# Moving three gradient half-pieces into the last spectral pair and two norm quarters, with x1's gradient in a tile of its own

## The chip, the cores and the metric

The kernel runs on one core of one Trainium2 chip. The metric is the device time of the whole program in microseconds (us), the median over several runs. Engines: TensorE (PE) multiplies matrices, VectorE (DVE) and ScalarE (ACT) work elementwise, GpSimd (POOL) and SyncE (SP) issue the DMAs here.

## The reference, cut to what matters

The program computes one transformer-like block and its full gradient: the output, and the gradients of x, two spectral filters, W1, b1, W2, b2, the conditioning vector c and the modulation matrix.

```python
mod = (_silu(c) @ w_mod).reshape(c.shape[0], 6, 1, -1)
sa, ca, ga, sb, cb, gb = ...
h = _layernorm(x, axis=-1) * (1 + ca) + sa
x = x + ga * _A_ref(h, A_w_r, A_w_i)          # rfft2, times a complex filter, irfft2
h = _layernorm(x, axis=-1) * (1 + cb) + sb
x = x + gb * _B_ref(h, B_w1, B_b1, B_w2, B_b2) # layernorm, W1, gelu, W2
...
_out, _vjp = jax.vjp(_f, A_x, A_w_r, A_w_i, B_w1, B_b1, B_w2, B_b2, c, w_mod)
_grads = _vjp(grad_out)
```

S = 2048 tokens, D = 1024 channels, F = 3584 hidden channels; everything that is stored is bf16.

## The kernel before

The kernel keeps 128 tokens or channels on the partitions. Both Fourier transforms are matrix products with cosine and sine tables. Symmetry splits each into four classes (CE, SE, CO, SO: even and odd cosines and sines), and the token axis is worked in four quarters of 512 tokens that are folded onto one another.

The forward part and the MLP's backward part come first; the change lies in the last 270 us. There `spectral_core(False, ...)` runs the spectral block backward:

- `s_fwd` makes four tables U with the token-axis products.
- Eight pairs follow (`pair(n, ...)`). Each multiplies its frequencies with the filters on VectorE and writes two rows groups of R. After pair n the callback `beside_bwd(n)` runs. Pair 7 completes R.
- `s_inv` makes the inverse token-axis products (L565, named `pv`): CE and SE after pair 5, CO and SO after pair 7. They read the tables smA2 and smB2 (tags `sma`, `smb`) and R.
- Four quarters i follow. The `po` products (L630) of a quarter are 32 small matmuls, evicted by L635 and L637 into `o4`, a slice of the tile `ct`. Then `consume_bwd(i, ...)` unfolds `o4` (L173), loads x's rows into `n1` (a tile `xt`, two of them in turn, tags `sma` and `px0`), normalises them on ScalarE (`norm_act`, L461), takes the layer norm backward row group by row group (L1185 and `ln_bwd`, L1032 to L1037), loads the gradient that comes from x1 into `n1` again (L1188), adds it (L1189) and stores the result (`store_tok`: one DMA on SP and two indirect ones on POOL).

Independent work for TensorE is laid between these steps by hand. `pieces()` is a generator: each `next` writes down one piece, and `fill(n)` draws n of them. A piece is 16 matmuls of 128x512: half of a 128-row block of W2's gradient (L1071, named `gw2acc`), or a 128x512 block of W1's gradient (L1252, named `gw1acc`). Numbered from 0 in the order of drawing, pieces 0 to 47 are W2 halves, pieces 48 to 51 are the last four W2 halves, cut by token quarter so that each frees one of the tiles gB, and pieces 52 to 107 are W1 blocks. Some pieces also write down loads: those of W2 load the hidden activations two blocks ahead (`hh_load`, L1214, a transposing DMA), and piece 52 loads the normalised tokens (`n3n`, L1237, into the tags t0 to t3 that the pairs' temporaries held) and calls `gw1_load` twice (L1203). Each `gw1_load` is two transposing DMAs of 1 MB into two of the four tiles `gzh`, which take the places of the four gB tiles. Every eighth W1 piece calls it again for the group after the next.

Drawn before the change: 12 pieces ahead of the pairs, 32 beside them (`fill(1)` four times per pair), 8, 8, 10 and 10 in the quarters (`fill((6, 6, 8, 8)[i])`, the column sums `halves_sum` on TensorE (L196), `fill(2)`), 8 with each of three modulation-gradient rows (`gmod_row`), and 4 at the end.

The tile framework's scheduler does not keep the written order strictly. Among instructions of one engine that it holds to be ready it takes the one written first; a tile that shares a tag waits until the last reader of the tile before it is done. `tc.issue_after(ins)` puts instructions behind `ins` on its engine. SP and POOL run their queues in order: an instruction that waits holds up all behind it.

Of the kernel before, what the change touches and what calls it, by code (L numbers as in the profile page):

```python
# [11 lines left out]
BF16 = mybir.dt.bfloat16  # L12
I32 = mybir.dt.int32
ACT = mybir.ActivationFunctionType
ALU = mybir.AluOpType
AX = mybir.AxisListType

P = 128
S = 2048
D = 1024  # L20
# [15 lines left out]
def kernel(  # L36
# [24 lines left out]
    nc = tc.nc  # L61
# [4 lines left out]
    reg = ctx.enter_context(tc.tile_pool(name="reg", bufs=1))  # L66
# [6 lines left out]
    def ps_s(name):  # L73
        return psum.tile([P, 512], FP32, tag="s", name=name)
# [31 lines left out]
    d_gx1 = dram.tile([S, D], BF16, name="d_gx1")  # L106
# [13 lines left out]
    def chunk_rows(dt, i):  # L120
        return dt[4 * i * P:4 * (i + 1) * P, :].rearrange("(q p) d -> p q d", p=P)

    def tok_flat(ap):
        return ap[0] if len(ap.shape) == 3 else ap

    def load_tok(t4, src, i, eng=None):
        s3 = tok_flat(src)
        ins = (eng or nc.sync).dma_start(out=t4[:, 0:4:3, :],
                          in_=bass.AP(tensor=s3.tensor, offset=s3.offset + 128 * i * D, ap=[[D, P], [1024 * D, 2], [1, D]]))
        for q in range(2):  # L130
            nc.gpsimd.indirect_dma_start(out=t4[:, 1 + q, :], out_offset=None, in_=s3,
                                         in_offset=bass.IndirectOffsetOnAxis(ap=xidx[:, 2 * i + q:2 * i + q + 1], axis=0))
        return ins
# [11 lines left out]
    def store_tok(dst, t4, i):  # L145
        s3 = tok_flat(dst)
        nc.sync.dma_start(out=bass.AP(tensor=s3.tensor, offset=s3.offset + 128 * i * D, ap=[[D, P], [1024 * D, 2], [1, D]]),
                          in_=t4[:, 0:4:3, :])
        for q in range(2):
            nc.gpsimd.indirect_dma_start(out=s3, out_offset=bass.IndirectOffsetOnAxis(ap=xidx[:, 2 * i + q:2 * i + q + 1], axis=0),  # L150
                                         in_=t4[:, 1 + q, :], in_offset=None)
# [20 lines left out]
    def tt(out, a, b, op):  # L172
        return nc.vector.tensor_tensor(out=out, in0=a, in1=b, op=op)  # L173
# [24 lines left out]
    def halves_sum(acc, src4, first, last):  # L198
        for i in range(4):
            for h in range(2):  # L200
                strip_sum(acc, h + 2 * (i % 2), src4[:, i, h * KH:(h + 1) * KH], first and i < 2, last and i >= 2)
# [7 lines left out]
    def store_halves(acc, row, spent4, r):  # L209
        odd = spent4[0:64, 0, :].bitcast(FP32)  # L210
        nc.scalar.copy(out=odd, in_=acc[64:128, :])
        tt(row, acc[0:64, :], odd, ALU.add)
        store_strips(row, 0, r)
# [63 lines left out]
    def unfold_d(o4, tmp):  # L277
        n = o4.shape[1]
        ov = o4.rearrange("p c (a b w) -> p c a b w", b=2, w=256)
        tv = tmp.rearrange("p c (s b w) -> p c s b w", s=2, w=256)  # L280
        tt(tv[:, :, 0], ov[:, :, :, 0, :], ov[:, :, :, 1, :], ALU.add)
        tt(tv[:, :, 1], ov[:, :, :, 0, :], ov[:, :, :, 1, :], ALU.subtract)
        fwd = o4.rearrange("p c (b w) -> p c b w", w=512)[:, :, :, 0:256]
        rev = bass.AP(tensor=o4.tensor, offset=o4.offset + 1023, ap=[o4.ap[0], [D, n], [-512, 2], [-1, 256]])
        tt(fwd, tv[:, :, :, 0, :], tv[:, :, :, 1, :], ALU.add)
        tt(rev, tv[:, :, :, 0, :], tv[:, :, :, 1, :], ALU.subtract)

    def unfold_tok(o4, tmp):
        tt(tmp[:, 0:4:2, :], o4[:, 0:4:2, :], o4[:, 1:4:2, :], ALU.add)
        tt(tmp[:, 1:4:2, :], o4[:, 0:4:2, :], o4[:, 1:4:2, :], ALU.subtract)  # L290
        tt(o4[:, 0:4:3, :], tmp[:, 0:2, :], tmp[:, 2:4, :], ALU.add)
        tt(o4[:, 1:3, :], tmp[:, 0:2, :], tmp[:, 2:4, :], ALU.subtract)
# [165 lines left out]
    def norm_act(out4, in4, row, i):  # L458
        for q in range(4):
            t = 4 * i + q  # L460
            nc.scalar.activation(out=out4[:, q, :], in_=in4[:, q, :], func=ACT.Identity,  # L461
                                 scale=stats[:, row, 0, t:t + 1], bias=stats[:, row, 1, t:t + 1])
# [567 lines left out]
    def ln_bwd(g_in, gsum, n_ap, rstd, out_ap, tmp):  # L1030
        sc = small.tile([P, 4], FP32, tag="lbsc", bufs=4)
        nc.vector.tensor_tensor_reduce(out=tmp, in0=g_in, in1=n_ap, scale=1.0, scalar=0.0,  # L1032
                                       op0=ALU.mult, op1=ALU.add, accum_out=sc[:, 1:2])
        nc.vector.tensor_scalar(out=sc[:, 2:3], in0=gsum, scalar1=rstd, scalar2=-1.0 / D, op0=ALU.mult, op1=ALU.mult)
        nc.vector.tensor_scalar(out=sc[:, 3:4], in0=sc[:, 1:2], scalar1=rstd, scalar2=-1.0 / D, op0=ALU.mult, op1=ALU.mult)
        nc.scalar.activation(out=tmp, in_=n_ap, func=ACT.Identity, scale=sc[:, 3:4], bias=sc[:, 2:3])
        nc.vector.scalar_tensor_tensor(out=out_ap, in0=g_in, scalar=rstd, in1=tmp, op0=ALU.mult, op1=ALU.add)  # L1037
# [127 lines left out]
    hh_o = [None, None] + [4, 5, 6, 7, 4, 5] + [0, 1] + [2, 0, 1] * 6  # L1165
    css2 = reg.tile([P, 2, 2, 2 * PW], BF16, name="cs01b", tag="px0")
    nc.gpsimd.memset(css2[:], 0.0)
    accCA = []

    def consume_bwd(i, o4, tmp, tmp2, n1):  # L1170
        if i == 0:
            accCA.append(ps_s("accCA"))
            nc.vector.tensor_copy(out=sacc, in_=o4[:, 0, :])
        else:
            tt(sacc, sacc, o4[:, 0, :], ALU.add)
        unfold_d(o4, tmp)
        unfold_tok(o4, tmp)
        load_tok(n1, A_x, i)
        with tc.issue_after(last_po[0].ins):
            norm_act(n1, n1, 0, i)  # L1180
        tt(tmp, o4, n1, ALU.mult)
        s1c = small.tile([P, 4], FP32, tag="s1c")
        for q in range(4):
            t = 4 * i + q
            nc.vector.tensor_tensor_reduce(out=o4[:, q, :], in0=o4[:, q, :], in1=opca_row, scale=1.0, scalar=0.0,  # L1185
                                           op0=ALU.mult, op1=ALU.add, accum_out=s1c[:, q:q + 1])
            ln_bwd(o4[:, q, :], s1c[:, q:q + 1], n1[:, q, :], stats[:, 0, 0, t:t + 1], o4[:, q, :], tmp2[:, q, :])
        nc.sync.dma_start(out=n1, in_=chunk_rows(d_gx1, i))  # L1188
        tt(o4, o4, n1, ALU.add)  # L1189
        store_tok(out_1, o4, i)  # L1190
        fill((6, 6, 8, 8)[i])
        halves_sum(accCA[0], tmp, i == 0, i == 3)
        fill(2)
        if i == 3:
            rows = small.tile([P, D], BF16, tag="gmrow", bufs=1)
            store_halves(accCA[0], rows[0:64, 0:KH], tmp, 1)
# [10 lines left out]
    def gmod_row(r, ins):  # L1207
        with tc.issue_after(ins.ins):
            for _ in gmod_steps(r, w1g["wr"], w1g["gw"], w1g["gr"][:, r % 2, :]):
                pass  # L1210
# [52 lines left out]
    def fill(n):  # L1263
        for _ in range(n):
            next(todo)
        done[0] += n
# [21 lines left out]
    def beside_bwd(n):  # L1288
        for k in range(4):
            fill(1)  # L1290
            if 3 - k < (1, 2, 2, 2, 2, 2, 3, 3)[n]:
                with tc.issue_after(hh_in[0].ins):
                    next(rows34)

    spectral_core(False, fbuf2, (smA2, smB2), em2, [css2[:, 0], css2[:, 1]],
                  new_pair_temps(["t0", "t1", "t2", "t3"]), act_copy, s_copy, act_copy, consume_bwd, "fr", pfs, fill, mid_bwd, beside_bwd)


# [7 lines left out]

    for r in (2, 1, 0):
        gmod_row(r, w1g["ins"])
        fill(8)
    fill(NFC * 4 - done[0])  # L1310
    fin2 = reg.tile([P, 2, P], BF16, name="fin2", tag="gm")
    make_identity(nc, fin2[:, 0, :])
# [40 lines left out]
```

## Time and profile before

| | us |
|---|---|
| median of 3 runs | 1466.65 (1458.96, 1466.65, 1467.49) |
| the profiled execution, its own time | 1469.58 |
| its span, first to last instruction | 1467.6 |
| TensorE busy | 1397.0 (95%) |
| VectorE busy | 1073.8 (73%) |
| ScalarE busy | 718.0 (49%) |
| GpSimd busy | 365.7 (25%) |
| mean granted TensorE clock | 0.987 |

The lines of a timeline give the start and length in us, engine, source line, operation, the tile written and the tiles read, a count, and in brackets the engine's idle time before it with what ended that. Lines of windows give for a stretch its length, then the busy time and count of PE, PEld (weight loads), DVE, ACT and POOL, then the granted TensorE clock as a share of full speed, the busy share of the DMA engines and GB/s. A line of waits has the total, the number of waits and the longest.

### The profile page before, as it was taken

How to read it: one execution, taken by the hardware profiler on the slowest of the kernel's cores; microseconds unless marked ns; L12 is line 12 of the kernel's file. 1: busy time of each engine (PE TensorE's matmuls, PEld its weight loads, DVE VectorE, ACT ScalarE, POOL GpSimd, SP SyncE). 2: the span in 40 equal slices, each digit the busy share in tenths (PEclk: the TensorE clock that was granted, in tenths of full speed). 3: DMA queues.
4: the chain of work that ended last, by engine and by line, in shares of the span. 5: the costliest groups of instructions: out<-in, count | busy, mean ns of one | idle time of the engine just before them, and what ended most of it. 6: DMA issues, size and time to landing. Idle time of an engine off the chain costs nothing. (4 is left out here: it accounts for less than half of the span.)

```text
span 1467.6 us, 18265 instructions
## 1 busy us (share of the span) xinstructions
PE 1397.0 (95%) x6703; PEld 652.8 (44%) x6835; DVE 1073.8 (73%) x1581; ACT 718.0 (49%) x953; POOL 365.7 (25%) x441
## 2 busy tenths in 40 slices
PE   5889999999999999999989999999999999899997
PEld 2434545444444434444434444444444445444443
DVE  5883787898799787887520789888467578898542
ACT  4765556757886666665302333342623434444211
POOL 6610541211112122122211011021245431222432
PEclk8999999999999999999999999999999999999999
DMA  9972573899886876696999275396699987766992
GB/s 333 284 229 58 145 243 131 267 240 333 243 252 219 248 247 226 209 293 210 241 306 253 82 261 183 120 267 170 186 223 256 255 212 215 196 180 179 290 249 103
DMA packets 358366, 324.27 MB, mean 221 GB/s; under 512 B 209386, under 2 KB 301056, under 8 KB 358022
## 3 DMA queue, kind: packets, MB, share of 16 engines
q1 hardware_dynamic: 324166, 207.71, 52.1%
q0 software_dynamic: 34112, 115.41, 22.6%
q8 instruction: 53, 0.87, 0.2%
q14 instruction: 35, 0.29, 0.1%
HBM read 162.06 MB, written 111.20 MB: 186 GB/s over the span
## 5 line engine op out<-in xcount | busy, mean ns | idle before, releaser
L684 PE MATMUL pp<-gBoT,wt 128*128 128x512 bf16 x878 | 197.4, 381 | 5.7 <-DMA wt<-in_B_w_dram 2.7
L948 PE MATMUL pg<-w1T,gzr 128*128 128x512 bf16 x876 | 194.6, 379 | 1.6 <-ACT gn3b L956 0.2
L1252 PE MATMUL gw1acc<-gzh,n3n 128*128 128x512 bf16 x876 | 194.0, 379 | 1.2 <-DMA gzh<-d_gz 0.2
L802 PEld LDWEIGHTS <-w 128*128 128x128 bf16 x896 | 87.3, 98 | 111.7 <-issue 7.6
L684 PEld LDWEIGHTS <-wt 128*128 128x128 bf16 x896 | 87.9, 98 | 110.0 <-issue 5.2
L948 PEld LDWEIGHTS <-gzr 128*128 128x128 bf16 x896 | 86.8, 98 | 107.8 <-issue 4.7
L1252 PEld LDWEIGHTS <-n3n 128*128 128x128 bf16 x896 | 87.6, 98 | 105.3 <-issue 1.9
L802 PE MATMUL pz<-n3Ta,w 128*128 128x512 bf16 x437 | 98.8, 381 | 6.0 <-DVE w2sD L873 2.7
L1071 PE MATMUL gw2acc<-gB,hhsA 128*128 128x512 bf16 x438 | 97.6, 379 | 1.9 <-ACT gwo L1078 1.3
L802 PE MATMUL pz<-n3Tb,w 128*128 128x512 bf16 x439 | 98.5, 379 | 0.5
L851 PEld LDWEIGHTS <-hhA 128*128 128x128 bf16 x608 | 59.9, 99 | 78.3 <-issue 10.0
L811 ACT ACTIVATE gt<-gt 128x2048 bf16<-128x2048 bf16 x28 | 53.5, 1910 | 72.3 <-DVE gt L173 72.3
L805 ACT ACTIVATE gt<-pz,b_col 128x512 bf16<-128x512 f32 x112 | 72.8, 684 | 29.6 <-PE pz L802 27.8
L173 DVE TENSOR_TENSOR gt<-gt,gt 128x2048 bf16<-128x2048 bf16 x56 | 68.5, 1224 | 21.6 <-ACT gt L813 20.9
L1256 ACT CAST gwo<-gw1acc 128x512 bf16<-128x512 f32 x50 | 29.1, 584 | 112.6 <-PE gw1acc L1252 91.1
L1078 ACT CAST gwo<-gw2acc 128x512 bf16<-128x512 f32 x46 | 26.8, 584 | 109.6 <-PE gw2acc L1071 80.0
L173 DVE TENSOR_TENSOR ct<-ct 128x2048 bf16<-128x2048 bf16 x64 | 75.9, 1218 | 2.0 <-DMA d_n<-ct 1.2
L992 DVE CUSTOM_DVE_ANT_0 otl<-otl 128x1024 bf16<-128x1024 bf16 x24 | 29.0, 1223 | 52.7 <-DMA otl<-in_w_mod_dram 47.1
L1071 PEld LDWEIGHTS <-hhsA 128*128 128x128 bf16 x448 | 43.7, 98 | 53.3 <-DMA hhsA<-d_hh 1.8
L807 ACT ACTIVATE gt<-gt 128x2048 bf16<-128x2048 bf16 x28 | 53.4, 1908 | 0.6
L813 ACT ACTIVATE gt<-gt 128x2048 bf16<-128x2048 bf16 x28 | 53.4, 1907 | 0.5
L1257 POOL DMA_DIRECT2D out_dram<-gwo x56 | 30.9, 553 | 81.9 <-ACT gwo L1256 47.2
(321 smaller groups left out, 2516.4 us busy)
## 6 DMA issues: line engine op xcount, KB each, us to landing
gzr<-d_gz SPq DMA_DIRECT2D x28, 512.0 KB
wblk<-in_w_mod_dram SPq DMA_DIRECT2D x12, 1024.0 KB
out_dram<-otl POOLq DMA_DIRECT2D x48, 256.0 KB
out_dram<-gwo POOLq DMA_DIRECT2D x96, 128.0 KB
d_ph<-pho POOLq DMA_DIRECT2D x21, 512.0 KB
d_hh<-hhA POOLq DMA_DIRECT2D x19, 512.0 KB
w2sD<-in_B_w_dram SPq DMA_DIRECT2D x14, 512.0 KB
hhC<-d_ph SPq DMA_DIRECT2D x14, 512.0 KB
```

The costliest lines, as they stand in the source:

```text
L173: return nc.vector.tensor_tensor(out=out, in0=a, in1=b, op=op)
L684: last_pe[0] = nc.tensor.matmul(pp[:], lhsT=wt[:, fg % 2, cch, k * P:(k + 1) * P], rhs=gBoT[j][:, cch, :], start=(cch == 0), stop=(cch == ...
L802: last_pe[0] = nc.tensor.matmul(pz[:], lhsT=w1s[g][:, cch, k * P:(k + 1) * P], rhs=n3T[:, cch, :], start=(cch == 0), stop=(cch == NDC - 1))
L805: nc.scalar.activation(out=zb[:, k, :], in_=pz[:], func=ACT.Identity, bias=b1_col[:, fc:fc + 1], scale=1.0)
L807: nc.scalar.activation(out=av, in_=zb, func=ACT.Square)
L811: nc.scalar.activation(out=sg, in_=bv, func=ACT.Sigmoid, scale=2.0 * GK)
L813: nc.scalar.activation(out=bv, in_=bv, func=ACT.Sigmoid, scale=-2.0 * GK)
L851: last_pe[0] = nc.tensor.matmul(pbs[i][:], lhsT=hh[:, k, i * P:(i + 1) * P], rhs=wp[:, k, :], start=False, stop=(g == 6 and k == 3))
L948: last_pg[0] = nc.tensor.matmul(pgs[i][:], lhsT=gzs[b, g][:, k, i * P:(i + 1) * P], rhs=w1Ts[g][:, k, h * KH:(h + 1) * KH], start=(g == 0 ...
L1071: nc.tensor.matmul(acc[:], lhsT=hh_of(fc)[:, t, :], rhs=gBs[t // 4][:, t % 4, h * KH:(h + 1) * KH], start=(t == 0), stop=(t == NT - 1))
L1252: nc.tensor.matmul(acc[:], lhsT=n3ns[t // 4][:, t % 4, cch * P:(cch + 1) * P], rhs=gz2[t // 8][:, t % 8, :], start=(t == 0), stop=(t == NT ...
L1257: nc.gpsimd.dma_start(out=out_4[cch * P:(cch + 1) * P, fg * 512:(fg + 1) * 512], in_=ob)
```

## The change

Piece 44 is drawn right after pair 7's four. Quarters 0 and 1 draw nine pieces each in place of eight. The three modulation rows draw seven each in place of eight. The load of x1's gradient goes into a tile of its own, `gx`, under the tag `smb` that smB2 held, is written down right behind the load of x, and is no longer made to wait for `n1`.

```diff
-    accCA = []
+    accCA, gxt = [], []
...
         if i == 0:
             accCA.append(ps_s("accCA"))
+            gxt.append(reg.tile([P, 4, D], BF16, name="gx", tag="smb"))
...
         load_tok(n1, A_x, i)
+        nc.sync.dma_start(out=gxt[0][:], in_=chunk_rows(d_gx1, i))
         with tc.issue_after(last_po[0].ins):
             norm_act(n1, n1, 0, i)
...
-        nc.sync.dma_start(out=n1, in_=chunk_rows(d_gx1, i))
-        tt(o4, o4, n1, ALU.add)
+        tt(o4, o4, gxt[0][:], ALU.add)
         store_tok(out_1, o4, i)
-        fill((6, 6, 8, 8)[i])
+        fill((7, 7, 8, 8)[i])
...
             if 3 - k < (1, 2, 2, 2, 2, 2, 3, 3)[n]:
                 with tc.issue_after(hh_in[0].ins):
                     next(rows34)
+        if n == 7:
+            fill(1)
...
     for r in (2, 1, 0):
         gmod_row(r, w1g["ins"])
-        fill(8)
+        fill(7)
```

## The prediction

> **What bounds the kernel now.** I read the page's busy table first, then the waits of TensorE from 1190 us on, then the timeline of TensorE and of the SP queue over the same stretch, then the granted clock, then the last 70 us.
>
> ```profile
> PE 1397.0 (95%) x6703; PEld 652.8 (44%) x6835; DVE 1073.8 (73%) x1581; ACT 718.0 (49%) x953; POOL 365.7 (25%) x441
> ```
>
> TensorE is busy 95% of the span, and no other engine is near it. A matmul that only changes place is worth nothing; what can be won is time in which TensorE stands still or runs slowly. Everything that the diff touches lies after 1190 us, where TensorE waited so (total us, times, longest):
>
> ```profile
> PE po L630 <- ACT ct L635: 3.2, 2, 3.0
> PE pv L565 <- DVE R L173: 2.2, 1, 2.2
> PE po L630 <- DVE ct L635: 1.1, 1, 1.1
> PE gw1acc L1252 <- DMA gzh<-d_gz: 0.2, 1, 0.2
> ```
>
> About 7 us in 270 us. The timeline shows where (start, length, instruction; idle time before it in brackets):
>
> ```profile
> 1196.42 0.81 PE L565 MATMUL pv<-smB,R 128*128 128x512 bf16 x3
> 1199.46 15.03 PE L565 MATMUL pv<-smB,R 128*128 128x512 bf16 x60 [2.22 <-DVE R L173]
> 1214.32 3.66 PE L630 MATMUL po<-gm,V 128*128 128x256 bf16 x32
> ...
> 1239.40 6.85 PE L1071 MATMUL gw2acc<-gB,hhsA 128*128 128x512 bf16 x31 [0.16 <-issue]
> 1246.09 1.47 PE L630 MATMUL po<-gm,V 128*128 128x256 bf16 x12
> 1248.69 2.08 PE L630 MATMUL po<-gm,V 128*128 128x256 bf16 x16 [1.13 <-DVE ct L635]
> 1251.00 1.02 PE L1252 MATMUL gw1acc<-gzh,n3n 128*128 128x512 bf16 x3 [0.22 <-DMA gzh<-d_gz]
> ...
> 1279.71 1.47 PE L630 MATMUL po<-gm,V 128*128 128x256 bf16 x12
> 1281.02 0.59 PE L1252 MATMUL gw1acc<-gzh,n3n 128*128 128x512 bf16 x2
> 1284.61 2.53 PE L630 MATMUL po<-gm,V 128*128 128x256 bf16 x12 [3.00 <-ACT ct L635]
> ```
>
> The reader sees three weak places: the inverse products of the odd classes wait for R of the last pair; the po products of quarter 1 and of quarter 2 wait for evictions, which stand behind VectorE's layer-norm work of the quarter before.
>
> Two of the gaps cost more than their length. The granted clock just behind them, the column after POOL, is half:
>
> ```profile
> 1199.80:1203.30 3.50, 3.50 (x10) 1.18 (x8) 3.36 (x6) 1.29 (x3) 1.08 (x2) 0.51 1.17 246
> 1285.00:1288.60 3.60, 3.38 (x15) 2.15 (x15) 2.15 (x4) 2.54 (x5) 0.46 (x1) 0.53 0.81 269
> ```
>
> I therefore price a stage by its length less its clean length. The odd inverse products take 1214.32 - 1196.42 = 17.90 us; the even ones took 14.14 (1151.16 to 1165.30): **3.76 lost**. A clean po stage is quarter 0's, 1214.32 to 1218.03: 3.71. Quarter 1 takes 6.20 (1246.09 to 1252.29), less 0.65 for three gw1 matmuls inside it (0.216 each): **1.84 lost**. Quarter 2 takes 10.21 (1279.71 to 1289.92), less 1.51 for seven: **4.99 lost**. Quarter 3 loses 0.36. Beyond the bare waits, the two large ones hold 1.54 and 1.77 us: the price of one half-clock spell, about 1.6.
>
> **The change, part by part.** A piece is 16 matmuls; ScalarE's evictions of the W1 products late in the run stand 3.45 us apart, so a piece is 3.45 us. Counting pieces from 0 in the order in which they are drawn, 44 are drawn by the end of pair 7 before, 45 after; by the end of quarters 0 to 3 it was 52, 60, 70, 80 and becomes 54, 63, 73, 83; after the three modulation rows both have 104. So 3 x 3.45 = 10.4 us of matmuls leave the end and come back earlier: zero in work.
>
> *Piece 44 ahead of the odd inverse products.* The last pieces end at 1196.42; one more ends at 1199.87, and R is there at 1199.46. It covers the 2.22 us wait, and with it the half-clock spell: 3.76 gained (between 0, if R moves too, and 3.76). Its operand hh 24 was issued on SP at 1186.75. The load of hh 26 that piece 44 issues is later than that on SP anyway, at 1209.35: 0.
>
> *One more piece in quarters 0 and 1.* They push the po products of quarter 2 back against VectorE's chain of quarter 1. That chain ran from the unfold at 1257.50 to about 1286.4, 29 us; TensorE would have 3.7 + 9 x 3.45 + 0.6 = 35.4 us between the starts of the two po stages instead of 31.9. The 3.00 us wait and its half clock go: 4.99 gained (0 to 4.99).
>
> *But piece 52 crosses the po products of quarter 1.* Piece 52 is the first of the W1 gradient. It issues four n3n loads (already on SP from 1195 on) and four transposing loads of gz, into buffers that pieces 48 to 51 free:
>
> ```profile
> 1235.28 12.46 SPq L1203 DMA_TRANSPOSE gzh<-d_gz  x3
> 1247.82 0.53 SPq L1188 DMA_DIRECT2D xt<-d_gx  x1
> 1248.45 8.98 SPq L1203 DMA_TRANSPOSE gzh<-d_gz  x1
> ```
>
> The first goes out when piece 48 ends (1235.1), the third, which piece 52 reads first, leaves SP at 1247.74, and piece 52 starts at 1251.00 on its landing: 15.9 us after the end of piece 48. In that time TensorE had pieces 49 to 51 (10.4), the halves sum (0.6) and quarter 1's po products (3.7): 14.7. Afterwards fill(7) draws 45 to 51 and fill(2) draws 52 and 53, so piece 52 stands ahead of those po products: cover 11.0, a new wait of 15.9 - 11.0 = 4.9. By rows the gaps of 2.22 and 3.00 were each followed by a half-clock spell and that of 1.13 was not, so this one pays 1.6 more: **6.5 lost**. Queued behind it on TensorE are piece 53 and quarter 1's po products, and behind those VectorE's unfold of quarter 1. These po products then find VectorE free: their 1.84 is gained. Bounds for the place: 1.8 lost (the scheduler puts the po products first and the old stall stays) to 6.5.
>
> The Trainium skill ("TensorE: Matmul & The Clock Gate", Part 1: The HAM clock gate) has the clock fall after an idle window of about 3.4 us; in this trace gaps of 2.22 and 3.00 already did it, so the measurement decides. By that page of the Trainium skill alone the old spells would not hang on those gaps and would stay, while the new gap would surely cost one; the sum below would lose 3.3.
>
> *x1's gradient in a tile of its own.* Four loads of 1 MB as before. The old one waited for the tile xt, VectorE stood 4.3 us for it in all (1.51 in quarter 0, 2.80 in quarter 2), TensorE not at all: 0, covered by the pieces; without that cover 1.5 to 2.8 a quarter. The new tile takes smB's place, free when the odd inverse products end (1214.3); SP is inside a transpose until 1217.41, so SP does not wait for it. It then runs beside an n3n load and hh 27; a gradient load lands in 5.95 us (the chain of waits, at 1323.00), and hh 27 was issued 6.7 us ahead of piece 48: 0, at worst 2. From quarter 1 on the load waits for the add of the quarter before; behind it on SP stand gz, x loads and stores, none wanted within 20 us.
>
> *The end.*
>
> ```profile
> 1402.76 17.32 SPq L1203 DMA_TRANSPOSE gzh<-d_gz  x2
> 1439.68 20.02 PE L1252 MATMUL gw1acc<-gzh,n3n 128*128 128x512 bf16 x90
> 1459.63 0.22 PE L188 MATMUL ptr<-fin,gc_bf 128*8 128x128 bf16 x1
> ```
>
> The span still ends 8 us behind the last matmul. The modulation rows start up to 6 us later while TensorE ends 4 us earlier; the last gz group is on chip by about 1421 and wanted at 1459.6 - 8 x 3.45 = 1432: 11 us of slack for 10. Cost 0, at worst 2.
>
> **Sum**: 3.76 + 4.99 + 1.84 - 6.5 = 4.1 us won. The profiled execution took 1469.58 us (span 1467.6 and 2.0 around it), so it would become 1465.5; it lies 2.9 above the median of the runs shown, 1466.65, so I predict **1462.5**.
>
> **Rivals.** (a) Forecast, 0.50. (b) *The new wait hardly appears*: the scheduler moves quarter 1's po products ahead of piece 52. For it: before, it set three gw1 matmuls between po groups. Against: these products need evictions that stand behind ScalarE's and VectorE's layer-norm work. Loss 1.8 instead of 6.5: 8.8 won, 1457.9; 0.20. (c) *The change does not cover R*: piece 44 is ordered behind the inverse products, which the diff's place does not forbid. Without the 3.76, 1466.3; 0.15. (d) *Slower*: SP takes a gradient load for quarter 1 ahead of the transpose that piece 52 reads. That load waits for VectorE's add, at about 1249.6; then 0.5 for it, 4.2 for the transpose, 3.3 to land: piece 52 at 1257.6, TensorE free at 1242.1, so 15.5 + 1.6 = 17.1 lost against 10.6 won, 1473.2. It decides as soon as that load stands ahead on SP. For it: SP already held a gradient load between two gz transposes. Against: gz is drawn earlier; 0.10. (e) *The half-clock spells do not hang on these gaps*: the old ones stay elsewhere, 3.3 less won, 1465.8. Against: the waits of 2.70, 2.75 and 4.34 us that end at 328, 530 and 738 us are followed by the same spell; 0.05. (This is what the Trainium skill's page on the clock gate makes of gaps under 3.4 us.)
>
> **How the numbers follow.** All of (a), (b), (c) and (e) lie within 1% of 1466.65 (1452.0 to 1481.3; 1% is about what a measurement of this kernel can tell from no change), and (d) too. The three runs of before spread from 1458.96 to 1467.49, which is larger than the effect: the range is 1453 to 1471, from (b) less 5 for that spread to just short of (d). Faster by over 1% needs all 10.6 and a low run: 0.07. Slower needs (d) and late modulation rows: 0.05. Same: 0.88.
>
> **What would show it.** Right: no wait for R ahead of the odd inverse products and none of 3 us in quarter 2's po products, a gw1 matmul waiting about 5 us for gzh near 1242 with half clock behind it, VectorE waiting for no gradient load, last matmul about 1455.5. Wrong: the po products of quarter 1 ahead of the first gw1 matmul (b), an SP queue standing at a gradient load while gz waits (d), or TensorE waiting for gzh in the last 60 us.

## The result: 0.76% slower

Over 22 runs each, the changed kernel takes 1476.37 us (median, 1467.19 to 1488.12) and the kernel before 1465.90 us (1458.96 to 1475.28): a ratio of 1.0076, 95% interval 1.0061 to 1.0091. The forecast was 1462.5, a little faster; the range ended at 1471. The profiled execution of the changed kernel took 1484.82 us (span 1483.0), 15.2 more than the profiled one before and 8.4 above its own median, so its stages show the loss at a large size.

In the profile after, TensorE is as busy as before in share, and it still bounds the kernel:

```profile
PE 1406.1 (95%) x6835; PEld 652.4 (44%) x6835; DVE 1074.2 (72%) x1582; ACT 717.1 (48%) x952; POOL 369.9 (25%) x441
```

Its waits from 1190 us on have changed entirely (total us, times, longest):

```profile
PE pv L565 <- ACT V L647: 11.3, 1, 11.3
PE gw1acc L1253 <- DMA gzh<-d_gz: 7.0, 2, 4.3
```

The wait for R and the waits for po evictions are gone, as intended. A wait of 11.3 us stands in their place: the odd inverse products wait for ScalarE to evict their own results (V). TensorE's timeline of the changed kernel:

```profile
1190.34 10.52 PE L1071 MATMUL gw2acc<-gB,hhsA 128*128 128x512 bf16 x48
1200.70 1.89 PE L565 MATMUL pv<-smB,R 128*128 128x512 bf16 x8
1213.93 14.67 PE L565 MATMUL pv<-smB,R 128*128 128x512 bf16 x56 [11.34 <-ACT V L647]
1228.44 3.66 PE L630 MATMUL po<-gm,V 128*128 128x256 bf16 x32
...
1256.74 1.37 PE L630 MATMUL po<-gm,V 128*128 128x256 bf16 x11
1262.44 8.75 PE L1253 MATMUL gw1acc<-gzh,n3n 128*128 128x512 bf16 x32 [4.32 <-DMA gzh<-d_gz]
1271.03 2.20 PE L630 MATMUL po<-gm,V 128*128 128x256 bf16 x17
...
1305.42 3.58 PE L630 MATMUL po<-gm,V 128*128 128x256 bf16 x28
...
1447.31 27.75 PE L1253 MATMUL gw1acc<-gzh,n3n 128*128 128x512 bf16 x120 [2.63 <-DMA gzh<-d_gz]
```

Three pieces (x48, pieces 42 to 44) run ahead of the inverse products, which no longer wait for R. Two groups of four matmuls run, and then TensorE stands until the PSUM buffers that they filled are evicted. What ScalarE did meanwhile, in its timeline of the same kernel:

```profile
1187.13 0.59 ACT L1078 CAST gwo<-gw2acc 128x512 bf16<-128x512 f32 x1 [2.14 <-PE gw2acc L1071]
...
1197.49 0.59 ACT L1078 CAST gwo<-gw2acc 128x512 bf16<-128x512 f32 x1 [2.87 <-PE gw2acc L1071]
1212.81 0.59 ACT L1078 CAST gwo<-gw2acc 128x512 bf16<-128x512 f32 x1 [14.73 <-DMA out_dram<-gwo]
1213.29 1.08 ACT L647 CAST V<-pv 128x512 bf16<-128x512 f32 x2
```

The eviction at 1212.81 is that of piece 44. It waits 14.7 us for a store, and the V evictions stand behind it in ScalarE's queue. The late W2 pieces evict into four half rows in turn (`gwo[:, fc % 2]`, two halves each), so piece 44 needs the half row of piece 40 back. Piece 40 was evicted at 1187.13. GpSimd's timeline shows its store, the first of the two issued from 1198.95 on, and the chain of waits how long that took to land:

```profile
1197.02 1.93 POOL L131 DMA_INDIRECT xt<-in_A_x_dram,xu  x1 [0.30 <-issue]
1198.95 1.15 POOL L1080 DMA_DIRECT2D out_dram<-gwo  x2
```

```profile
1198.95 13.76 DMA out_dram<-gwo
...
1212.81 0.59 ACT gwo L1078
```

The store was issued 11.2 us after the eviction, because it stood on GpSimd's queue behind other transfers and what these waited for, and took 13.76 us to land. In the kernel before, piece 44 was evicted only in quarter 0, near 1222, by VectorE, and did not wait for the half row. The stall also keeps the clock at half (the figure after POOL's), and for longer than the spells before:

```profile
1205.20:1218.90 13.70, 4.97 (x12) 1.72 (x12) 0.00 (x0) 2.73 (x5) 0.00 (x0) 0.50 1.11 228
```

### The profile page after: what moved, and what is told of

Read it like the earlier page. It is cut to its first block, busy times and chain, and to the rows that moved or that the text cites. A ratio compares the mean times of both kernels' runs of the same rounds, so it can differ in the third digit from the quotient of the medians.

```text
span 1483.0 us, 18398 instructions
## 1 busy us (share of the span) xinstructions
PE 1406.1 (95%) x6835; PEld 652.4 (44%) x6835; DVE 1074.2 (72%) x1582; ACT 717.1 (48%) x952; POOL 369.9 (25%) x441
## 4 chain that ended last, share of the span: by engine, by line
PE 40%; DVE 20%; DMA 9%; ACT 6%; issue 6%; POOL 1%; SPq 1%; POOLq 0%; DVEq 0%; ACTq 0%
PE gw2acc L1071 9%; PE gw1acc L1253 9%; PE pbo L851 7%; PE pz L802 5%; PE pg L948 5%; DVE gt L173 4%; PE pu L472 2%; DVE got L1032 2%; PE pv L565 2%; DVE ct L173 2%; DMA out_dram<-otl 1%; ACT ct L461 1%; DVE gn3a L1037 1%; DVE st L437 1%; DMA out_dram<-gwo 1%
## 5 line engine op out<-in xcount | busy, mean ns | idle before, releaser
L1253 PE MATMUL gw1acc<-gzh,n3n 128*128 128x512 bf16 x896 | 198.8, 384 | 7.0 <-DMA gzh<-d_gz 7.0
L173 DVE TENSOR_TENSOR gt<-gt,gt 128x2048 bf16<-128x2048 bf16 x56 | 68.5, 1223 | 21.6 <-ACT gt L813 20.9
L992 DVE CUSTOM_DVE_ANT_0 otl<-otl 128x1024 bf16<-128x1024 bf16 x24 | 29.0, 1222 | 56.7 <-DMA otl<-in_w_mod_dram 50.7
```

The source lines that it names most:

```text
L1253: nc.tensor.matmul(acc[:], lhsT=n3ns[t // 4][:, t % 4, cch * P:(cch + 1) * P], rhs=gz2[t // 8][:, t % 8, :], start=(t == 0), stop=(t == NT ...
```

## The experiments

Two theories stood at the start. **Q**: the loss is ScalarE's queue, as just read. **D**: the loss is DMA traffic, the gradient load and the gz transposes that come earlier. All ratios are to the kernel before. SP's timeline of the changed kernel already speaks against D: both loads are issued only after the wait of 11.3 us, which ended at 1213.93.

```profile
1228.63 0.37 SPq L1180 DMA_DIRECT2D gx<-d_gx  x1
...
1245.94 19.74 SPq L1204 DMA_TRANSPOSE gzh<-d_gz  x4
```

**Without piece 44 beside pair 7**

```diff
-        if n == 7:
-            fill(1)
```

> The change without piece 44 beside pair 7; quarters 0 and 1 still draw nine pieces each and the gradient tile stays; the piece that is left over is drawn at the end. Theory Q (the loss is ScalarE's queue: piece 44's eviction waits for its output row to be stored, and the V evictions stand behind it): the odd inverse stage is back at about 17.9 us, ScalarE has no wait of over 5 us on the output store there, and the time falls by about 10 us against the changed kernel, to within 4 us of the kernel before. Theory D (the loss is DMA traffic: the gradient load, the n3n loads and the gz transposes that come earlier): the inverse stage keeps a wait of 5 us or more and the time stays 8 us or more above the kernel before. Both expect the wait of about 4 us for gzh at the first gw1 matmul, since piece 52 is still drawn ahead of quarter 1's po products.

Measured: 1.0018 (0.9997 to 1.0038), some 8.5 us below the changed kernel. The inverse stage takes 18.56 us and waits for R again (2.9 us), ScalarE has no wait for a store there, and the first gw1 matmul waits 6.9 us for gzh. The wait for gzh is longer than the 4 us that were expected. Q holds: one piece of 3.45 us carries most of the loss.

**Piece 44 in a row of its own**

```diff
+        if (fc, h) == (24, 0):
+            spare = small.tile([P, D], BF16, name="spare", tag="gmrow", bufs=1)
+            with tc.high_priority():
+                nc.any.tensor_copy(out=spare[:, half], in_=acc[:])
+            nc.gpsimd.dma_start(out=out_6[fc * P:(fc + 1) * P, half], in_=spare[:, half])
+            return
```

> The changed kernel, with piece 44 alone evicted into a row of its own (a free 2 KB tile) instead of the row that piece 40's store still reads; nothing else. Theory Q: the wait of ScalarE for the output store goes, the inverse stage takes about 14.5 us (no wait for R either, no half clock), 11 to 13 us less than the 27.7 of the changed kernel's profile, and the time is some 3 us below the kernel before, 10 to 13 below the changed one. Theory D: the inverse stage still waits, on the V evictions or on R, and the time stays within 3 us of the changed kernel.

Measured: 1.0005 (0.9980 to 1.0031), some 10 us below the changed kernel. TensorE's timeline:

```profile
1185.17 10.52 PE L1071 MATMUL gw2acc<-gB,hhsA 128*128 128x512 bf16 x48
1195.53 13.98 PE L565 MATMUL pv<-smB,R 128*128 128x512 bf16 x64
1209.34 3.66 PE L630 MATMUL po<-gm,V 128*128 128x256 bf16 x32
...
1239.05 1.38 PE L630 MATMUL po<-gm,V 128*128 128x256 bf16 x11
1245.89 8.46 PE L1259 MATMUL gw1acc<-gzh,n3n 128*128 128x512 bf16 x32 [5.46 <-DMA gzh<-d_gz]
```

All 64 inverse products run without a gap: 13.81 us from their start to the po products, where the kernel before needed 17.90 and the changed one 27.74. Q is shown: the piece, its place and its traffic are the same, only the half row is not. But the 3 us below the kernel before that were expected did not show. By the profile quarter 1 loses 7.2 us (the kernel before lost 1.84), with 5.46 us of wait for gzh and a half-clock spell, and hh 27 costs 1.2; against that stand 4.1 us won at the inverse products and 4.8 in quarter 2. Some 2 us should be left, which the interval neither shows nor excludes.

**Piece 44's eviction on VectorE**

```diff
-            nc.any.tensor_copy(out=row[:, half], in_=acc[:])
+            (nc.vector if (fc, h) == (24, 0) else nc.any).tensor_copy(out=row[:, half], in_=acc[:])
```

> The changed kernel, with piece 44's eviction alone put on VectorE, which has nothing to do between pair 7 and quarter 0's first eviction; it still waits for the same output row. Theory Q says that the wait costs only because the V evictions stand behind it on ScalarE: TensorE's wait of 11.3 us goes although VectorE now shows the wait of some 10 to 14 us, and the time is 9 to 12 us below the changed kernel, as with the row of its own. If a late row cost by itself, the time would stay within 3 us of the changed kernel.

Measured: 1.0036 (1.0017 to 1.0056), some 6 us below the changed kernel, less than the 9 to 12 expected. VectorE now waits for the store, and TensorE does not:

```profile
DVE gwo L1078 <- DMA out_dram<-gwo: 3.9, 1, 3.9
```

The inverse stage takes 13.84 us. That a late row costs only what is queued behind its eviction holds. The wait is 3.9 us and not 14.7 for two reasons: VectorE came free only at 1201.17, some 4 us after piece 44's end, and the store, issued at 1195.32, landed by 1205.0, within 9.7 us and not 13.76. So the lateness itself differs from profile to profile. The runs' median lies above that of the version with the row of its own, but the two intervals overlap; the profile has 6.5 us of wait for gzh.

**Piece 40's store from ScalarE's queue**

```diff
+            eng = nc.scalar if (fc, h) == (22, 0) else nc.gpsimd
-            nc.gpsimd.dma_start(out=out_6[fc * P:(fc + 1) * P, half], in_=row[:, half])
+            eng.dma_start(out=out_6[fc * P:(fc + 1) * P, half], in_=row[:, half])
```

> The changed kernel, with the store of piece 40's output row issued from ScalarE's queue right behind its eviction instead of from GpSimd's queue, where it stood 11 us behind other transfers before it was issued (evicted by 1187.7, issued at 1198.95, landed at 1212.71). If GpSimd's queue is what makes the row late, the store lands 9 to 12 us earlier, ScalarE waits 0 to 5 us in place of 14.7, TensorE's wait ahead of the inverse products falls from 11.3 to 0 to 2 us, and the time is 8 to 11 us below the changed kernel. If the busy DMA engines alone make it late, a store issued 11 us earlier among the same traffic still lands near 1208 or later: ScalarE waits 8 us or more and the time stays within 4 us of the changed kernel.

Measured: 1.0014 (0.9992 to 1.0037), some 9 us below the changed kernel. ScalarE's timeline shows the store right behind its eviction, and piece 44's eviction without a wait for it:

```profile
1185.19 0.59 ACT L1078 CAST gwo<-gw2acc 128x512 bf16<-128x512 f32 x1 [2.17 <-PE gw2acc L1071]
1185.80 0.41 ACTq L1081 DMA_DIRECT2D out_dram<-gwo  x1
...
1198.95 0.58 ACT L1078 CAST gwo<-gw2acc 128x512 bf16<-128x512 f32 x1 [2.87 <-PE gw2acc L1071]
```

The store landed within the 13.2 us to 1198.95; how long it took is not shown. Without the time on GpSimd's queue the row is back in time.

**Piece 52 behind quarter 1's po products**

```diff
-        fill((7, 7, 8, 8)[i])
+        fill((6, 8, 8, 8)[i])
         halves_sum(accCA[0], tmp, i == 0, i == 3)
-        fill(2)
+        fill((1, 2, 2, 2)[i])
```

> The changed kernel, but quarter 0 draws seven pieces (45 to 51) and quarter 1 ten, so that piece 52 stands behind quarter 1's po products as in the kernel before. Both theories: the wait of 4.3 us for gzh at the first gw1 matmul and its half clock go, about 5 us; in their place quarter 1's po products may wait 1 to 4 us for evictions. Theory Q: ScalarE's wait for the output store and TensorE's 11 us ahead of the inverse products stay as they are, and the time is 1 to 5 us below the changed kernel, still 5 us above the kernel before. Theory D: with gz out of the way the larger part of the 10 us goes.

Measured: 1.0068 (1.0045 to 1.0091), not distinguishable from the changed kernel. ScalarE waits 13.9 us for the store, TensorE 10.2 ahead of the inverse products. The wait for gzh shrank only from 4.3 to 3.2 us, where it was expected to go: SP still takes the transposes when piece 48 ends (1238.88), and they land late even behind the po products. So this run did not move the transposes, and says little on D; with the row of its own, where the traffic is the same and the wait is gone, D falls.

**The gradient tile alone**

> Only the gradient tile of its own; all pieces drawn as in the kernel before. Theory Q: VectorE's 4.3 us of waits for the gradient go, VectorE's chain ends 2 to 3 us earlier in each quarter, and the 3.0 us wait of quarter 2's po products with its half clock shrinks or goes: 0 to 4 us faster than the kernel before. Theory D: the gradient load beside n3n and hh 27 makes hh 27 or gz late: 2 to 6 us slower than the kernel before.

Measured: 0.9999 (0.9975 to 1.0022). VectorE's waits for the gradient and TensorE's wait of 3.0 us in quarter 2 went (0.3 and 0.2 us are left there), as Q expected; against that TensorE waited 2.6 us for hh 27 and 4.9 for gzh, as D expected. These roughly cancel. But this profile is the slowest of the version's twelve runs, 10 us above their median, so it shows which waits come and go, not their usual size.

**Seven pieces in quarter 0, the row of its own, without and with the gradient tile**

```diff
-        fill((6, 6, 8, 8)[i])
+        fill((5, 7, 8, 8)[i])
...
+        if n == 7:
+            fill(1)
```

> The kernel before, with piece 44 beside pair 7 and evicted into a row of its own, seven pieces in quarter 0 (45 to 51), nine in quarter 1, and the gradient loaded into x's tile as before; piece 52 stays behind quarter 1's po products. If the stages add up as the profiles have them: 3.8 us won at the inverse products, up to 5.0 at quarter 2's po products, no new wait for gzh over 1 us: 4 to 9 us faster than the kernel before. If the gain at the inverse products is given back at the next wait (hh 27 or gzh, which follow the end of piece 45 and 48), it is within 2 us of the kernel before.

> The same with the gradient tile of its own, loaded early as in the changed kernel. If the early load beside hh 27, n3n and gz makes these late, a wait of 1 to 3 us for hh 27 or of 3 to 5 us for gzh comes back and it is 2 to 5 us slower than the version without the tile; if the load is harmless, the two agree within 1.5 us.

Measured: 0.9997 (0.9976 to 1.0017) and 1.0013 (0.9991 to 1.0034). Without the tile the profile has only 2.3 us of wait for gzh and 2.2 for evictions left, and yet the runs show no gain: 4 to 9 us were expected if the stages add up, and what came is the other branch, within 2 us of the kernel before. What took the rest was not found. With the tile TensorE waits 3.4 us for hh 27. Over all the profiles of this case, hh 27 made TensorE wait (1.2 to 4.0 us) in six of the nine versions with the tile and in none of the five without it. Piece 48 is the first that reads hh 27, and the gz transposes start when it ends, so such a wait delays them as well.

**The gz tiles laid the other way round**

Piece 52 reads tiles 0 and 1. Tile 0 stood in the place that piece 50 frees, so it was the third transpose of the chain. Now tiles 0 and 1 stand where pieces 48 and 49 end:

```diff
-        w1g["gz"] = [reg.tile([P, 8, 512], BF16, name=f"gzh{k}", tag=PXT[2 + k]) for k in range(4)]
+        w1g["gz"] = [reg.tile([P, 8, 512], BF16, name=f"gzh{k}", tag=PXT[(3, 4, 2, 5)[k]]) for k in range(4)]
```

> The changed kernel with piece 44's row of its own, and with the gz tiles laid the other way round: the two that piece 52 reads stand where pieces 48 and 49 end first, so that the second transpose and not the third is the one it waits for. Theory: what the cover at the inverse products won was given back at piece 52, whose gz load starts only when piece 48 ends; one transpose (about 4.5 us) less in that chain takes the 5.5 us wait of the version with the row of its own down to 0 to 2 us and its half-clock spell away: 4 to 7 us below that version, 3 to 9 us faster than the kernel before. Rival (the gain is lost in the tail, at the modulation rows and the last gz groups, or in the spread of the runs): within 3 us of the kernel before, with a wait for gzh in the last 60 us.

> The same as the version with the row and the gz order, but x1's gradient goes into x's tile as in the kernel before. If the early gradient load is what makes hh 27 late (1.2 to 3.4 us in four of the versions so far), the wait for hh 27 goes and it is 1 to 4 us faster than with the tile; VectorE waits for the gradient again, 2 to 5 us in all, which costs TensorE nothing while nine pieces stand beside it.

> The version with the row of its own, seven pieces in quarter 0, nine in quarter 1 and the gradient in x's tile, with the gz order. Its wait of 2.3 us for gzh and the half clock go; the wait of 1.6 us for evictions in quarter 2 may stay: 2 to 4 us below the version without the gz order and 3 to 6 us faster than the kernel before. Rival: within 2 us of the kernel before.

> The kernel before with the gz order alone, as a control. Its piece 52 waited 0.2 us: 0 to 1 us, within the interval of no change. If it is faster by 3 us or more, the order is worth something for another reason than piece 52's wait.

Measured: the changed kernel with its own row and this order 0.9957 (0.9936 to 0.9978), 6 us faster than the kernel before and the only version whose interval lies wholly below 1; the same without the gradient tile 1.0008 (0.9989 to 1.0027); seven pieces in quarter 0 with the order 1.0001 (0.9975 to 1.0028); the order alone 0.9995 (0.9967 to 1.0023). In the fastest version piece 52 no longer waits, though piece 48 waits 4.03 us for hh 27 and a later W1 piece 2.54 us for gzh:

```profile
1228.14 14.85 PE L1071 MATMUL gw2acc<-gB,hhsA 128*128 128x512 bf16 x56 [4.03 <-DMA hhsA<-d_hh]
1242.92 0.61 PE L196 MATMUL accCA<-ct,ones_bf 128*32 128x512 bf16 x8
1243.47 7.08 PE L1259 MATMUL gw1acc<-gzh,n3n 128*128 128x512 bf16 x32
```

Without the tile this version is 0.5% slower, against the expectation, which had it faster. VectorE's waits in the version without it suggest why:

```profile
DVE ct L173 <- DMA xt<-d_gx: 17.4, 4, 6.7
```

Four waits, up to 6.7 us each, where the kernel before had two of 4.3 in all; why they grew was not tried. VectorE's chain ends late, and TensorE waits 7.1 us for evictions in that profile. The reading is that VectorE's chain is the next bound once TensorE's own gaps are closed, and that the tile counts there; no run tests it by itself. The version with seven pieces in quarter 0 missed the 3 to 6 us that were expected of it: its profile has no wait for gzh left, but 4.5 us for evictions, 3.7 of them in quarter 2.

## Why the prediction was wrong, step by step

*The step that failed: piece 44 ahead of the odd inverse products, the term of 3.76 us won.* The prediction counted its matmuls, its operand and the load that it writes down, and gave the bounds 0 to 3.76 us won. It left out the rest of the piece: an eviction and a store into a ring of four half rows. The moved eviction was ahead of V's in ScalarE's queue, and its row was not free. In place of 3.76 won the stage lost 27.74 - 17.90 = 9.8 us: ScalarE waited 14.7 us for the row, and TensorE 11.3 us for ScalarE. No reason had been given for excluding a loss, and the range ended below the result for that. The cover itself worked as said: with the row out of the way the stage took 13.81 us, 4.1 less than before.

*Piece 52 crossing the po products: right, in place and size.* In the changed kernel the stretch from 1256.74 to 1274.12 holds quarter 1's po products (3.71 when clean) and 34 gw1 matmuls (7.3); 17.38 - 3.71 - 7.3 = 6.3 us lost, where 6.5 was forecast for the new wait. The scheduler did part of (b) too: eleven recorded po matmuls (three groups, 1.4 us) ran first. They hardly shortened the wait, 4.3 us where 4.9 was forecast, because the transposes landed 16.7 us after the end of piece 48 and not 15.9. No po product of quarter 1 waits for an eviction any more, so the 1.84 is gained as forecast: 4.5 lost in all, 4.7 by the forecast.

*Quarter 2: right.* From 1305.42 to 1310.21, less four gw1 matmuls (0.9) and 3.71: 0.2 lost instead of 4.99, so 4.8 won.

*The gradient tile at 0: right alone (0.9999), wrong as a rule.* The worst case of 2 us for hh 27 was too small (up to 4.0), and in the fastest version the tile is worth 0.5%.

*The end at 0, at worst 2: past its worst case.* The profile after has a second wait for gzh, 2.63 us up to 1447.31, with a half-clock spell of some 1.6 behind it: 4.2 lost. The slack of 11 us rested on the time that the last pair of transposes took before. They kept SP for 28.09 us, against 17.32. That is no accident of this profile, as five other versions that draw seven pieces with a modulation row have 20.9 to 26.5 us there; the cause was not tried:

```profile
1416.08 28.09 SPq L1204 DMA_TRANSPOSE gzh<-d_gz  x2
```

*The sum.* Against the profile before: 9.8 lost at the inverse products, 6.3 - 1.84 = 4.5 at quarter 1, 4.8 won at quarter 2, 4.2 lost at the end: 13.7 of the 15.2 us between the two profiled executions. Two terms carry the miss, the inverse products (13.6 us off) and the end (4.2 us off). Over the median runs the loss is 10.5.

*The rivals.* The slower case (d), an SP queue standing at a gradient load, did not occur: SP took that load for quarter 1 at 1266.86, behind all four gz transposes. Slower came by an engine that the prediction had not looked at. (c) fell: R was covered. (e) did not come true: the two old half-clock spells went with their gaps, and new ones came behind the new gaps. The argument against it was thinner than it read, though: the profile before has a wait of 2.61 us that ends at 402.4 us with no spell behind it, so a gap of this size need not cost one.

## What to carry to other kernels

A piece of filler work is its matmuls, its eviction, its output row and its store; before it is moved, look up which queue its eviction joins, what stands behind it there, and when the row that it writes was last given back. Four half rows at 3.45 us a piece are a ring of 14 us, and a store that needs 11 us to be issued and 14 to land does not fit into it. And when one wait is covered, follow the chain that starts at the covered work (here the transposes that start when piece 48 ends), which may take the gain back. Of the versions tried, only one that also changed which buffer is freed first was clearly faster, and the other two that had this order and the free row were not.

## What the runs showed of the hardware

A 128 KB store issued at 1198.95 took 13.76 us to land, while the DMA engines were at a busy share of about 1 with transposes and 1 MB loads under way; in the version with the eviction on VectorE the same store took at most 9.7 us, at about the same share.

The half-clock spell lasted 13.7 us around the gap of 11.3: it goes on while TensorE stands. The spells that follow gaps of 2.2 to 4.3 us in the two first profiles, from 300 us on, last 3.4 us each. That is not a fixed price: behind the gap of 3.31 us in the version with piece 40's store on ScalarE's queue the spell lasted 6.8 us, and 10.2 us around the gap of 10.21 in the version with piece 52 later. These lengths are 3.4 us and about two, three and four times that. No length of gap decides alone whether a spell comes: gaps of 2.61 us (before, at 402 us), 2.40 (after, at 329 us) and 2.54 (the fastest version, in the last 60 us) had none behind them, and one of 1.56 us in the version with seven pieces and x's tile had one. The Trainium skill ("TensorE: Matmul & The Clock Gate", Part 1: The HAM clock gate) ties the return to full speed to about 3.4 us of sustained activity; the trace agrees roughly, the clock being back at 1218.9, some 5 us after the matmuls went on at 1213.93.
